# Pair chunks of a GLU kernel: seven products with the left-over rows stacked in, weight sums in another order, a PSUM bank seeded by a copy

## The chip, the cores and the metric

The kernel runs on one core of one Trainium2 chip. The metric is the time of one execution in microseconds (us); it is given as the median of several runs, and smaller is better. PE is the matrix engine (PEld its weight loads), DVE the vector engine, ACT the scalar engine, POOL the GpSimd engine (it issues the DMAs that add into DRAM), SP the sync engine (it issues most loads). Each engine works through its own queue in the order in which the program was laid out.

## The reference

```python
h  = x + A_ref(layernorm(x), wqkv, wo)          # attention over 8 dilated keys, 32 heads
def B_ref(x, w_gate, w_up, w_down):
    h = sigmoid(x @ w_gate) * (x @ w_up)        # x: 2048 x 576, F = 4608
    return h @ w_down
h2 = h + B_ref(layernorm(h), w_gate, w_up, w_down)
```

All is float32. The second half, the GLU, takes most of the time and is all that the change touches.

## The kernel before

**Precision.** A float32 operand is split into a high part (rounded to fp32r) and a low part (what is left), and a product of two operands is three matmuls: high times high, low times high, high times low. `split` (L103) is one ACT copy for the high part and one DVE subtraction for the low part.

**Tiling.** The 2048 tokens are four blocks of 512. F is cut into 36 pieces of 128. The contraction of 576 is 512 (four slabs of 128, two *halves* of two slabs) and a *rest* of 64. The rest's high and low parts are stacked on 128 partitions, so that a rest costs two matmuls (`rest`, L751) and not three.

**Chunks.** The list `items` has 84 chunks, numbered c: 12 single chunks of block 0, 24 *pair chunks* of blocks 0 and 1 (c = 12 to 35), 12 single chunks of block 2 (c = 36 to 47), and 36 pair chunks of blocks 2 and 3 (c = 48 to 83, "the last pair"). A pair chunk (`pair`, from L818 on) computes gate and up of both blocks with seven block products in place of eight: the blocks' halves are a00, a01 (first block), a10, a11 (second), and with sums s1 to s4 of them and sums t1 to t4 of the weights the products are b00, b10, t2, t3, t1, t4 and b11, each of six matmuls (`prod`, L742), accumulated in three PSUM banks b1, b2, b3. Four rests of two matmuls go with b10, t1, t4 and b11. That makes 50 matmuls of 512 columns a chunk. Between products, partial results are copied (ACT) or added (DVE), with a high priority; the gate of the first block is copied out of b1 (L824), the product b10 is added by DVE (L829), and ACT takes the sigmoid (L830).

**Work between the products.** `between(i)` puts other work after each product: down projections of earlier chunks, and one step of a background generator. In the last pair the down projection also has seven products (`down_seven`, L919): 42 matmuls of 288 columns a chunk, PSUM tile `dp`, evicted by ACT into `ev` (L936), and added to DRAM by a POOL DMA (L939). In single chunks `dp` is added to `stage` by DVE (L878).

**Weights.** `weights` (L712) makes the operands of chunk c+1 while chunk c runs: DVE sums (L727 to L730) into a tile `tw`, then splits into w1 (two buffers), w2, w3, w4 (one each). `load_gu` (L700) loads the raw weights of chunk c+2 into `wg` (two buffers, SP); it can start when the last reader of the buffer is done. `down_side` (L1153) loads the raw down weights `wd` of two chunks, splits them, and sums them.

**Operands of the last pair.** During the single chunks c = 36 to 47 the background generator makes blocks 2 and 3 of the GLU's input (`proj_scr`, tiles `ar` and `ar3`), and `operands` (L1014) then makes the sums (`sums`, L279) and their splits (`x_half`, L300) in a pool `pp2`, c = 45 to 46. At c = 48 the last two operands, s1 and a11, are split, `pp2` is closed, and `wd` takes its place in SBUF.

**Order.** No order is written out by hand: a scheduler places the instructions of all engines by its own estimates, with priorities (`tc.high_priority`) and pins (`tc.issue_after`). So an edit in one place can move instructions elsewhere.

## Time and profile before

| | |
|---|---|
| median of 3 runs | 1569.44 us (1567.49 to 1575.35) |
| profiled execution: span from first to last instruction | 1566.1 us (no other time is given for it) |
| single chunks of block 2 | about 746 to 938 us |
| last pair, c = 48 to 83 | about 938 to 1536 us, then the last down products |
| weights in wg of the last pair | 36 loads of 640 KB |

A row of a timeline reads: start in us, duration in us, engine, line, operation, out<-in, shape, count of merged instructions, and in brackets the idle time before it with what ended it. PE's ends are modelled (matmuls are pipelined), so PE is read by the distance from start to start. The same goes for DVE and ACT, where one instruction's end overlaps the next one's start by some 0.1 us.

### The profile page before, as it was taken

The numbers are of one execution on the slowest core, as the hardware profiler recorded it, in microseconds if no ns is written. First come the engines' busy times: TensorE is split into PE (matmuls) and PEld (weight loads), VectorE is DVE, ScalarE is ACT, GpSimd is POOL, SyncE is SP. The second block draws the span as 40 slices with busy tenths as digits, with TensorE's granted clock in tenths as the row PEclk, the third lists the DMA queues.
The fourth block names the chain that finished last, engine by engine and source line by source line (L and its number), as shares of the span: only waits on it lengthen the run. The fifth ranks groups of instructions, "written<-read, shape, count | busy, mean of one in ns | idle before, by whom it ended". The sixth has DMA issues, their size and how long they took to land.

```text
span 1566.1 us, 22356 instructions
## 1 busy us (share of the span) xinstructions
PE 1545.8 (99%) x8520; PEld 1374.2 (88%) x8520; DVE 1254.3 (80%) x1880; ACT 882.6 (56%) x1584; POOL 207.4 (13%) x252
## 2 busy tenths in 40 slices
PE   8999999999999999999999999999999999999998
PEld 7999988887888888888888988888888888888888
DVE  7998999979999999999536688866777776677754
ACT  6632344435566555665542355766777666677761
POOL 3300000011000010000101000121112112112212
PEclk9999999999999999999999999999999999999999
DMA  8646555366565775665683424998899989989983
GB/s 281 219 166 222 190 200 183 107 225 199 145 174 150 200 183 150 162 159 125 180 243 113 179 85 119 205 180 176 170 181 186 172 172 183 175 170 181 185 166 137
DMA packets 77148, 273.96 MB, mean 175 GB/s; under 512 B 8336, under 2 KB 14224, under 8 KB 76144
## 3 DMA queue, kind: packets, MB, share of 16 engines
q0 software_dynamic: 28192, 107.29, 37.4%
q1 hardware_dynamic: 41216, 145.11, 27.8%
q10 hardware_dynamic: 7632, 20.12, 3.3%
q8 instruction: 66, 1.08, 0.3%
q14 instruction: 42, 0.34, 0.1%
HBM read 143.98 MB, written 130.87 MB: 176 GB/s over the span
## 4 chain that ended last, share of the span: by engine, by line
PE 82%; DVE 10%; DMA 5%; ACT 2%; issue 1%; POOL 0%; SPq 0%; ACTq 0%; POOLq 0%; DVEq 0%
PE b L747 40%; PE dp L868 14%; PE dp L930 11%; PE b L754 8%; PE acc L157 4%; DMA wg<-in_wmlp_dram 2%; DVE pr L189 2%; DVE lg L193 1%; DVE pr L215 1%; PE b L157 1%; PE bgp L157 1%; DMA x<-tok 1%; DVE w L105 1%; DMA kw<-k 1%; DVE pr L221 1%
## 5 line engine op out<-in xcount | busy, mean ns | idle before, releaser
L747 PE MATMUL b<-tl,w 128*128 128x512 f32 x1692 | 429.6, 393 | 1.2 <-ACT s L824 0.6
L747 PEld LDWEIGHTS b<-tl,w 128*128 128x128 f32 x1692 | 305.8, 188 | 57.9 <-ACT tl L104 1.2
L747 PE MATMUL b<-th,w 128*128 128x512 f32 x1332 | 343.0, 392 | 0.5 <-DVE s L843 0.5
L747 PEld LDWEIGHTS b<-th,w 128*128 128x128 f32 x1332 | 242.7, 188 | 45.3 <-DVE s L843 0.9
L936 ACT ACTIVATE ev<-dp 128x576 f32<-128x576 f32 x224 | 145.0, 647 | 62.9 <-PE dp L930 58.6
L754 PE MATMUL b<-th,w 128*128 128x512 f32 x564 | 174.9, 391 | 0.0
L939 POOL DMA_DIRECT2D h<-ev x128 | 109.2, 853 | 459.4 <-ACT ev L936 445.6
L104 ACT ACTIVATE w<-wg 128x384 fp32r<-128x384 f32 (+1 forms) x186 | 111.0, 600 | 98.5 <-PE b L754 54.4
L157 PE MATMUL acc<-qw,th 128*128 128x432 f32 x512 | 154.5, 363 | 2.4 <-DVE th L109 2.3
L105 DVE TENSOR_TENSOR w<-wg,w 128x384 fp32r<-128x384 f32 (+1 forms) x186 | 121.0, 656 | 36.7 <-ACT w L104 36.5
L105 DVE TENSOR_TENSOR w<-tw,w 128x512 fp32r<-128x512 f32 x120 | 82.6, 688 | 81.6 <-ACT w L104 80.7
L754 PEld LDWEIGHTS b<-th,w 128*128 128x128 f32 x564 | 106.0, 188 | 23.0
L868 PE MATMUL dp<-d,h1h 128*128 128x288 f32 x640 | 118.8, 295 | 0.0
L868 PE MATMUL dp<-d,h0h 128*128 128x288 f32 x608 | 112.2, 295 | 0.0
L876 ACT ACTIVATE stage<-dp 128x576 f32<-128x576 f32 x104 | 66.9, 646 | 68.1 <-PE dp L868 67.8
L157 PEld LDWEIGHTS acc<-qw,th 128*128 128x128 f32 x512 | 96.9, 189 | 7.7 <-DVE th L109 3.1
L868 PEld LDWEIGHTS dp<-d,h1h 128*128 128x128 f32 x640 | 98.7, 189 | 3.0
L868 PEld LDWEIGHTS dp<-d,h0h 128*128 128x128 f32 x608 | 94.0, 189 | 3.5 <-DVE stage L878 0.3
L104 ACT ACTIVATE w<-tw 128x512 fp32r<-128x512 f32 x120 | 75.3, 628 | 35.7 <-PE b L747 34.6
L157 PE MATMUL acc<-qw,tl 128*128 128x432 f32 x256 | 92.8, 363 | 0.1
L189 DVE TENSOR_TENSOR pr<-kw,q 128x2304 f32<-128x2304 f32 x32 | 81.8, 2555 | 8.3 <-DMA kw<-k 8.1
L884 POOL DMA_DIRECT2D h<-stage x26 | 31.1, 1197 | 416.2 <-ACT stage L876 337.2
(323 smaller groups left out, 2969.6 us busy)
## 6 DMA issues: line engine op xcount, KB each, us to landing
h<-ev POOLq DMA_DIRECT2D x96, 576.0 KB, 7.3
wg<-in_wmlp_dram SPq DMA_DIRECT2D x47, 928.0 KB, 5.2
h<-stage POOLq DMA_DIRECT2D x26, 1152.0 KB, 11.6
wg<-in_wmlp_dram SPq DMA_DIRECT2D x36, 640.0 KB, 4.2
kw<-k SPq DMA_DIRECT2D x16, 792.0 KB, 4.6
vw<-v SPq DMA_DIRECT2D x16, 792.0 KB, 4.9
wd<-in_wmlp_dram SPq DMA_DIRECT2D x18, 576.0 KB, 7.2
h<-ev POOLq DMA_DIRECT2D x32, 288.0 KB, 6.8
```

What stands on the lines that cost most here:

```text
L104: act.activation(hi, src, AF.Copy)
L105: splits.append(dve.tensor_tensor(lo, src, f32(hi), ALU.subtract))
L157: pe.matmul(ps[:, :n], a[:, c, js], m[:, c], start=k == 0, stop=False)
L189: dve.tensor_tensor(pr, both(kw, u), q[:, us].unsqueeze(2).broadcast_to([P, 2, W, CG]), ALU.mult)
L747: pe.matmul(ps, wt[:, a, k0 + c], xx[:, m + c], start=first and k == 0, stop=k == 5, skip_group_check=True)
L754: pe.matmul(ps, wt[:, a, k0], xx[:, 4], start=False, stop=a == 1, skip_group_check=True)
L868: pe.matmul(ps[:, i, :DH2], a[:, js], d[:, m, i * DH2:(i + 1) * DH2], start=k == 0, stop=k == n)
L876: act.activation(hv, ps, AF.Copy)
L884: pool.dma_start(hacc[b], hs, accum_op=ALU.add, max_dma_last_dim=8 * D)
L930: pe.matmul(ps[:, i, :DH2], a[x][:, js], m[y], start=k in (0, 1, 3) and q == 0, stop=q == 2, skip_group_check=True)
L936: act.activation(hs[:, k % 2], ps[:, :, :DH2], AF.Copy)
L939: pool.dma_start(hsev[:, u, k0:k + 1], hs[:, :k + 1 - k0], accum_op=ALU.add, max_dma_last_dim=8 * D)
```

## The change

1. **49 matmuls.** In the last pair, the rest takes part in the seven products: each half of the contraction is now 256 + 32, the 32 rows stand four times on the 128 partitions (x: high, low, high, low; weights: high, high, low, low), so that one matmul gives all of it. Seven products of six, and seven rests of one: 49 matmuls. The weights come from a second array `wfull`, 1536 columns a chunk in place of 1280 (768 KB in place of 640 KB).
2. **Weight sums and splits of the last pair** (`full_weights`) are made in place in `wg`, in another order, over 384 columns each; the rests of t1 to t4 lie in one tile `tr`. Its first split (w1) is pinned on ACT behind the sigmoid of the chunk before.
3. **Operands of the last pair.** The rests of blocks 2 and 3 go through DRAM (`rscr`) and come back fourfold in sixteen POOL DMAs (`rr`), their sums are made separately (`sums_rest`, five DVE additions), and `x_full` splits all seven operands with their rests (`split_quads`: one ACT copy, two DVE subtractions on 32 partitions each). Before, three operands had a rest, with one subtraction each.
4. **Order of products and PSUM seeding, all pair chunks.** b00, t3, t2, b10, t1, t4, b11. Except in the first chunk of each pair (c = 12 and 48), ACT copies b00 into the bank of b10 (`b2`), b10 is accumulated on it, and ACT takes the sigmoid from there: the DVE addition of L829 is gone. The bank of b00 is the one that held b10 in the chunk before.
5. **The second block's gating** is placed ahead of b11 (`last(1, ...)`), the first one's behind it.
6. Buffers: `s` 3 (4), `ev` 3 (4), `d3` 1 (2).

```diff
+    def split_quads(t, src):
+        act.activation(t, src, AF.Copy)
+        for q in (32, 96):
+            dve.tensor_tensor(t[q:q + 32], src[q:q + 32], f32(t[q:q + 32]), ALU.subtract)
...
+    def sums_rest(q0, q1, s1):
+        (a00, a01), (a10, a11) = q0, q1
+        dve.tensor_tensor(s1, a10, a11, ALU.add)
+        yield
+        dve.tensor_tensor(a10, a00, a10, ALU.subtract)
+        yield
+        dve.tensor_tensor(a00, s1, a00, ALU.subtract)
+        yield
+        dve.tensor_tensor(a01, a01, a00, ALU.subtract)
+        yield
+        return dict(s1=s1, s2=a00, s3=a10, s4=a01, a11=a11)
...
+    def full_weights(ws):
...
+            w1 = gw.tile([P, 2, 5, P], F32R, bufs=2, name="w1")
+            with ExitStack() as way:
+                if c >= NF + NSTD:
+                    way.enter_context(tc.issue_after(added[1]))
+                act.activation(w1[:, :, 0:3], r[:, 2:4], AF.Copy)
...
+            dve.tensor_tensor(r[:, 1], r[:, 0], r[:, 1], ALU.subtract)
+            dve.tensor_tensor(r[:, 2], r[:, 1], r[:, 2], ALU.add)
+            dve.tensor_tensor(r[:, 3], r[:, 3], r[:, 2], ALU.subtract)
+            tr = gw.tile([P, 8, P], F32R, tag="tw", name="tr")
+            w2 = sum_pair("w2", 0, slice(1, 3))
...
+            act.activation(w4[:, 0:3], r[:, 0], AF.Copy)
...
+            dve.tensor_tensor(r[:, 0], r[:, 0], r[:, 2], ALU.subtract)
+            w3 = sum_pair("w3", 2, slice(0, 4, 3))
...
-        prod(b2, X["a01"], w, "b10", True)
-        rest(b2, X["a01"], w, "g4")
...
-            added[0] = dve.tensor_tensor(s1, s1, b2, ALU.add)
-            act.activation(s1, s1, AF.Sigmoid)
+        product(b1, "b00", "a00", w, True, ())
...
+            act.activation(b2 if clean else s1, b1, AF.Copy)
...
+        product(b3, "t3", "s3", w, True, ())
...
+        product(b1, "t2", "s2", w, False, ())
...
+        product(b2, "b10", "a01", w, not clean, (("a01", "g4"),))
...
+            if clean:
+                act.activation(s1, b2, AF.Sigmoid)
...
+            for i in range(2):
+                for h in range(2):
+                    a = rscr[i][32 * h:32 * h + 32, :]
+                    for q in range(4):
+                        pool.dma_start(rr[i][h][32 * q:32 * q + 32], a)
```

How the scheduler's order changes is shown at three places. The first is PE in the first chunk of the last pair (c = 48) and the start of the next. Before, from the product t1 of chunk 48 on (tl_9019 is s1, th_9022 is a11, th_8904 is s4, tl_8832 is a00):

```order
L747 MATMUL b1_9049<-tl_9019,w3_8941 128x512 x6
L754 MATMUL b1_9049<-th_9022,w4_8939 128x512 x2
L747 MATMUL b3_9051<-th_9022,w3_8941 128x512 x6
L754 MATMUL b3_9051<-th_9022,w1_8936 128x512 x2
L747 MATMUL b1_9049<-th_8904,w4_8939 128x512 x6
L754 MATMUL b1_9049<-th_8904,w4_8939 128x512 x2
L747 MATMUL b2_9212<-tl_8832,w1_9031 128x512 x6
```

After, from the product b00 of chunk 49 (bank b1_9258) on; xs3, xs2 and xs1 are the rests of s3, s2 and s1, tl_9047 is s1, th_9054 a11, th_8994 s4, tl_8970 s3:

```order
L822 MATMUL b1_9258<-tl_8859,w1_9064 128x512 x6
L832 MATMUL b1_9258<-xa00_8860,w1_9064 128x512
L832 MATMUL b3_9090<-xs3_8971,tr_8944 128x512
L822 MATMUL b3_9090<-th_9054,w3_8955 128x512 x2
L832 MATMUL b2_9089<-xs2_8988,tr_8944 128x512
L822 MATMUL b3_9090<-th_9054,w3_8955 128x512 x4
L822 MATMUL b2_9089<-tl_9047,w3_8955 128x512 x6
L832 MATMUL b2_9089<-xs1_9048,tr_8944 128x512
L832 MATMUL b3_9090<-th_9054,tr_8944 128x512
L822 MATMUL b2_9089<-th_8994,w4_8950 128x512 x6
L832 MATMUL b2_9089<-th_8994,w4_8950 128x512
L822 MATMUL b3_9259<-tl_8970,w2_9072 128x512 x6
```

Ahead of these rows PE has, from the start of chunk 48, b00 with its rest (7), the six of t3, the six of t2, and b10 with its rest (7), with 46 matmuls of `dp` between them. The rest matmuls of t3 and t2 have moved behind all of that and behind b00 of the next chunk.

The second place is DVE in chunk 48. Before, from the gating of the last single chunk (L767) to the rest of a11 (L109):

```order
L767 TENSOR_TENSOR s_8970<-s_8970,b2_8955 128x512
L878 TENSOR_TENSOR stage_7678<-stage_7678,dp_9005 128x576
L105 TENSOR_TENSOR h1l_9002<-s_8970,h1h_9001 128x512
L105 TENSOR_TENSOR w4_8939<-wg_8855,w4_8939 128x384
L105 TENSOR_TENSOR th_9022<-ar3_8328,th_9022 128x1024
L878 TENSOR_TENSOR stage_7678<-stage_7678,dp_9062 128x576
L105 TENSOR_TENSOR w1_9031<-wg_8952,w1_9031 128x640
L727 TENSOR_TENSOR tw_9037<-wg_8952 128x512
L829 TENSOR_TENSOR s_9052<-s_9052,b2_9050 128x512
L109 TENSOR_TENSOR th_9022<-ar3_8328,th_9022 64x512
```

After, the same gating (L850) is followed by nineteen rows (four of `stage`, two of 1024 columns, the weights of chunks 48 and 49 and the rest of a11 among them) and then by these; s_9092 is the gate of chunk 48, whose addition needs b10:

```order
L924 TENSOR_TENSOR s_9092<-s_9092,b1_9091 128x512
L107 TENSOR_TENSOR w2_9072<-wg_8960,w2_9072 128x2x256
L965 TENSOR_TENSOR stage_7657<-stage_7657,dp_9172 128x576
L770 TENSOR_TENSOR wg_9087<-wg_9087 128x384
L304 TENSOR_TENSOR rd_8815<-rr10_8818,rr11_8819 128x512
L306 TENSOR_TENSOR rr10_8818<-rr00_8816,rr10_8818 128x512
L116 TENSOR_TENSOR xs1_9048<-rd_8815,xs1_9048 32x512 x2
L116 TENSOR_TENSOR xs3_8971<-rr10_8818,xs3_8971 32x512 x2
L308 TENSOR_TENSOR rr00_8816<-rd_8815,rr00_8816 128x512
L310 TENSOR_TENSOR rr01_8817<-rr01_8817,rr00_8816 128x512
L116 TENSOR_TENSOR xs2_8988<-rr00_8816,xs2_8988 32x512 x2
L116 TENSOR_TENSOR th_8994<-rr01_8817,th_8994 32x512 x2
```

The sums and splits of the rests stand behind the addition that waits for b10. On ACT, in chunk 49, the split of the first down weights (d3<-wd) stands ahead of the first gating's copy (h0h) and of the seeding copy (L909).

The third place is DVE in every second chunk further on. Before, between the last read of a raw weight buffer (w4<-wg_12213) and the first read of the weights loaded into it (w1<-wg_12556) stood these rows:

```order
L105 TENSOR_TENSOR w4_12393<-wg_12213,w4_12393 128x384
L728 TENSOR_TENSOR tw_12546<-wg_12406,tw_12546 128x256
L105 TENSOR_TENSOR h0l_12526<-r00_12523,h0h_12525 128x512
L730 TENSOR_TENSOR tw_12546<-wg_12406,tw_12546 128x256
L829 TENSOR_TENSOR s_12561<-s_12561,b2_12559 128x512
L105 TENSOR_TENSOR w2_12544<-tw_12546,w2_12544 128x512
L843 TENSOR_TENSOR s_12563<-s_12563,b1_12558 128x512
L105 TENSOR_TENSOR d_12659<-wd_12236,d_12659 128x576
L848 TENSOR_TENSOR s_12562<-s_12562,b3_12560 128x512
L105 TENSOR_TENSOR w3_12545<-tw_12546,w3_12545 128x512
L105 TENSOR_TENSOR w1_12733<-wg_12556,w1_12733 128x640
```

After, the last read is tr<-wg_10231, and the first read of what is loaded into its place is the sum on wg_10584 (L770); s_10591 and s_10590 are the additions that wait for the products t1 and t4:

```order
L107 TENSOR_TENSOR w3_10424<-wg_10231,w3_10424 128x2x256
L753 TENSOR_TENSOR tr_10413<-wg_10231,tr_10413 64x256
L772 TENSOR_TENSOR wg_10429<-wg_10429 128x384
L107 TENSOR_TENSOR w2_10569<-wg_10429,w2_10569 128x2x256
L770 TENSOR_TENSOR wg_10584<-wg_10584 128x384
L929 TENSOR_TENSOR s_10591<-s_10591,b1_10586 128x512
L933 TENSOR_TENSOR s_10590<-s_10590,b3_10587 128x512
```

Only two rows are now left between the end of the buffer's use and the first read of its next load, and the additions stand behind that read.

More of the change, by code (lines that the diff above doesn't have):

```diff
@@ L45 @@
 GU = 10 * P
+GF = 12 * P
 WC = GU + D
@@ L60, with kernel @@
 @with_exitstack
-def kernel(ctx, tc, x, wqkv, wo, wmlp, out):
+def kernel(ctx, tc, x, wqkv, wo, wmlp, wfull, out):
     nc = tc.nc
@@ L298, in tl_tile, with x_full @@
         return xt.tile([P, 4, TB], F32R, tag="tl", bufs=4, name="tl")
+    def x_full(n, raw, rest):
+        if n in ("a01", "a11", "s4"):
+            t = th_tile()
+            r = t[:, 4]
+        else:
+            t = tl_tile()
+            r = xr.tile([P, TB], F32R, name="x" + n)
+        split(t[:, 0:2], t[:, 2:4], raw)
+        split_quads(r, rest)
+        XR[n] = r
+        return t
+    XR = {}
+    xr = None
     def x_half(raw, rest):
@@ L746, in prod, with product @@
             for a, m in ((0, 0), (0, 2), (1, 0)):
-                pe.matmul(ps, wt[:, a, k0 + c], xx[:, m + c], start=first and k == 0,
+                lhs = wt[:, a, k0 + c] if isinstance(k0, int) else wt[:, 2 * a + c]
+                pe.matmul(ps, lhs, xx[:, m + c], start=first and k == 0,
                           stop=k == 5, skip_group_check=True)
                 k += 1
+    def product(ps, n, xn, w, first, rests):
+        prod(ps, X[xn], w, n, first)
+        if isinstance(w[n][1], int):
+            for m, wn in rests:
+                rest(ps, X[m], w, wn)
+        else:
+            pe.matmul(ps, w[n][1], XR[xn], start=False, stop=True, skip_group_check=True)
     def rest(ps, xx, w, n):
@@ L849, in pair @@
             gated[0] = act.activation(s2, s2, AF.Sigmoid)
+            added[1] = getattr(gated[0], "ins", gated[0])
         between(5)
-        prod(b1, X["s4"], w, "b11", False)
-        rest(b1, X["s4"], w, "u4")
         with tc.high_priority(HC):
-            last((s1, b1), (s2, s3))
+            last(1, s2, s3)
+        product(b1, "b11", "s4", w, False, (("s4", "u4"),))
+        with tc.high_priority(HC):
+            last(0, s1, b1)
         between(6)
@@ L1292, in between @@
                 side(i)
-            pair(X, w, between, last)
+            pair(w, between, last)
         else:
@@ L1309, in between @@
                 down_side(f, i)
-            pair(X, w, between, last if f >= NF - NPL else last_sums(f))
+            pair(w, between, last if f >= NF - NPL else last_sums(f))
             if f < NF - NPL:
```

133 lines of the change are left out of this document (88 added, 45 removed).

## The prediction

> **What bounds the kernel now.** I read the page's busy line first, then PE's waits, then the windows by stage.
>
> ```profile
> PE 1545.8 (99%) x8520; PEld 1374.2 (88%) x8520; DVE 1254.3 (80%) x1880; ACT 882.6 (56%) x1584; POOL 207.4 (13%) x252
> ```
>
> A busy PE need not be a PE at its limit, so what it waits for is asked next. In the pair chunks it waited three times, 1.6 us in all:
>
> ```profile
> PE b L747 <- ACT s L824: 0.6, 1, 0.6
> ```
>
> ```profile
> PE b L747 <- DVE s L843: 0.5, 1, 0.5
> PE b L747 <- ACT tl L104: 0.5, 1, 0.5
> ```
>
> The windows of the last pair, its start and its long part. The columns are the length, then the busy time of PE, PEld, DVE, ACT and POOL with their instructions, the granted clock, the DMA share and GB/s:
>
> ```profile
> 938.00:985.00 47.00, 47.00 (x243) 40.63 (x241) 41.74 (x73) 26.15 (x48) 2.99 (x3) 1.00 0.53 134
> 985.00:1510.00 525.00, 525.00 (x2823) 458.72 (x2822) 376.90 (x651) 374.05 (x658) 104.88 (x123) 1.00 0.91 179
> ```
>
> The last pair is bound by PE from end to end, at the full clock. In its long part DVE has 28% to spare (377 of 525 us) and ACT 29%; in its first 47 us DVE has 11%. So a matmul less is time gained, and DVE work costs nothing in the long part but may cost at the start.
>
> **The change, part by part.** The sums below are made on the profiled execution (span 1566.1 us) and then taken off or put on the median of 1569.44, which lies 3.3 us above it.
>
> *49 matmuls.* The price of one is read from start to start, at the rests and in the product ahead of them:
>
> ```profile
> 1109.29 1.55 PE L747 MATMUL b<-tl,w 128*128 128x512 f32 x6
> 1110.67 0.62 PE L754 MATMUL b<-th,w 128*128 128x512 f32 x2
> 1111.14 0.29 PE L930 MATMUL dp<-d,h0h 128*128 128x288 f32 x1
> ```
>
> Six take 1.38 us, the two rests 0.47: 0.23 each. 36 chunks lose one each: 36 x 0.23 = **8.3 us less**. The rows of "128*128" do not say how many rows hold data, and the stacked rest is the same 128x512 as the old one, so it is priced alike. [...]
>
> *DVE addition gone, seeding.* Some 58 additions of 512 columns go. PE did not wait for them (rows above), so they are worth nothing by themselves; what covers them is PE's own work between b10 and the second gating. The seeding copy is as long as the copy that it replaces. It now waits for the gating of the chunk before, which reads its bank; between that chunk's b11 and the product t2, which needs the copy done, PE has b00, t3 and at least one `dp` group, over 3 us.
>
> *The start of the last pair.* Here the order was moved most. The rows around 938 us in the trace of before give the spacing of DVE's operations by size, where DVE ran without a gap:
>
> ```profile
> 934.87 0.69 DVE L105 TENSOR_TENSOR w<-tw,w 128x512 fp32r<-128x512 f32 x1
> 935.47 1.22 DVE L105 TENSOR_TENSOR tl<-rs,tl 128x1024 fp32r<-128x1024 f32 x1
> 936.61 0.68 DVE L767 TENSOR_TENSOR s<-s,b 128x512 f32<-128x512 f32 x1
> ...
> 938.66 0.55 DVE L105 TENSOR_TENSOR w<-wg,w 128x384 fp32r<-128x384 f32 x1
> 939.13 1.22 DVE L105 TENSOR_TENSOR th<-ar,th 128x1024 fp32r<-128x1024 f32 x1
> 940.27 0.75 DVE L878 TENSOR_TENSOR stage<-stage,dp 128x576 f32<-128x576 f32 x1
> 940.93 0.82 DVE L105 TENSOR_TENSOR w<-wg,w 128x640 fp32r<-128x640 f32 x1
> ...
> 958.58 0.43 DVE L728 TENSOR_TENSOR tw<-wg,tw 128x256 f32<-128x256 f32 x1
> 958.92 0.76 DVE L105 TENSOR_TENSOR d<-wd,d 128x576 fp32r<-128x576 f32 x1
> ```
>
> From start to start: 0.60 for 512 columns, 1.14 for 1024, 0.47 for 384, 0.66 for 576, 0.34 for 256. Half the partitions do not make it shorter:
>
> ```profile
> 942.98 0.69 DVE L109 TENSOR_TENSOR th<-ar,th 64x512 fp32r<-64x512 f32 x1
> ```
>
> so I price the new ones on 32 partitions at 0.60 too. Up to the last single chunk's gating (L767 at 936.61) both orders hold nearly the same DVE work, because the new operations ahead of it replace ones that have moved behind; I let it start at 936.7. From it to the split of the rest of s3 (xs3) the new order has 14 operations of 512 columns, 5 of 576, 2 of 1024, 5 of 384, 3 of 256 and one smaller: 8.4 + 3.3 + 2.3 + 2.4 + 1.0 + 0.2 = 17.6 us. So the rest of s3 is there at **954.3**.
>
> PE's work up to there is counted from the start of chunk 48:
>
> ```profile
> 936.64 1.54 PE L747 MATMUL b<-tl,w 128*128 128x512 f32 x6
> 938.02 0.42 PE L868 MATMUL dp<-d,h1h 128*128 128x288 f32 x2
> ...
> 939.61 1.54 PE L747 MATMUL b<-th,w 128*128 128x512 f32 x6
> ```
>
> Twelve `dp` matmuls take 939.61 - 938.02 = 1.59 us, 0.13 each. The new order gives PE 7 + 6 + 6 + 7 matmuls of chunk 48, b00 of chunk 49 (7) and 46 of `dp`: 33 x 0.23 + 46 x 0.1325 = 13.7 us, that is until **950.3**. Then it meets the rest of t3 and waits 4.0 us. Behind that it has three matmuls (0.7 us) until the rest of t2, for which DVE needs two sums and two splits, 2.4 us: 1.7 us more, until 956.7.
>
> A third wait follows in chunk 49. The first load of down weights (`wd`) began in the run of before as soon as the last split that read `pp2`'s space had ended (935.47 + 1.22):
>
> ```profile
> 936.76 0.90 SPq L1145 DMA_DIRECT2D wd<-in_wmlp_dram x2
> ```
>
> From the issue of these two to landing:
>
> ```profile
> DMA to landing us min/median/max: 3.9/4.4/4.9
> ```
>
> Now that space holds the fourfold rests, and the reader that ends last is the split of xs2, at 956.7. With 3.9 to 4.9 us to land (the answer just quoted, for these two transfers) the weights are there at 961. ACT's rows of 512 columns give its spacing:
>
> ```profile
> 956.04 0.60 ACT L824 ACTIVATE s<-b 128x512 f32<-128x512 f32 x1 [0.22 <-PE b L747]
> 956.53 0.62 ACT L104 ACTIVATE h0h<-r 128x512 fp32r<-128x512 f32 x1
> ```
>
> ACT wants the down weights at about 962.6: t4 ends at 959.7 (956.7 and 13 matmuls), then come two additions (1.2), the sigmoid and two weight copies at 0.55 each, an estimate from these two rows (0.49 from start to start, 0.60 alone). Behind the down weights stand the gating's copy and the seeding copy, done at 964.2. PE has finished b11 and t3 by 962.9 and wants to write t2 over the seeded bank: 1.3 us of waiting. Together 4.0 + 1.7 + 1.3 = **7.0 us more**.
>
> The bounds take the times from issue to landing by kind of transfer (median us, last column):
>
> ```profile
> h<-ev POOLq DMA_DIRECT2D x96, 576.0 KB, 7.3
> ...
> wg<-in_wmlp_dram SPq DMA_DIRECT2D x36, 640.0 KB, 4.2
> ...
> wd<-in_wmlp_dram SPq DMA_DIRECT2D x18, 576.0 KB, 7.2
> ...
> h<-hj POOLq DMA_DIRECT2D x12, 288.0 KB, 2.6
> ```
>
> At least: the rest of s3 cannot come before b10's end (947.1) and the eight rows from the addition to xs3 (ten operations, 5.9 us), 953.0, so 2.7 + 1.7 = 4.4 us. At most: the down weights land in the 7.2 us that all loads of `wd` take in the median and not in 3.9 (+1.3), and DVE comes 3 us later than I let it, since every one of its microseconds counts there: 11.5 us.
>
> ```profile
> 903.82 0.74 POOL L976 DMA_DIRECT2D h<-hj  x1 [2.04 <-DVE hj L262]
> ```
>
> ```profile
> 916.18 0.26 ACT L978 ACTIVATE ar<-bgp 128x128 f32<-128x128 f32 x1
> ```
>
> The sixteen POOL transfers are covered. The last column of `ar` is written at 916.44, a POOL issue takes 0.74, so the write and eleven loads behind it are out by 926; the nearest POOL transfers land 2.6 (h<-hj) to 7.3 us (h<-ev) later, over 12 us ahead of their first use on DVE (946).
>
> *The long part.* A chunk gets some 1.6 us more of DVE work on weights and loses 0.6; it has 4.8 us of DVE to spare (28% of a chunk's 17.1 us, which are 50 x 0.23 + 42 x 0.1325). The new rest tile and the in-place sums put the first read of a load two rows behind the end of the buffer's last use. 768 KB at the pace of 640 in 4.2 us take 5.0, so DVE stands for some 4 us at that sum. In the order shown third, the buffer's last use comes some 7.5 us after t4 of the chunk before: b11 ends 2.4 us after it (a `dp` group of 0.8, seven matmuls of 1.6), and eleven DVE rows follow (5 us). The addition behind the waiting sum needs t1, which ends 14.4 us after that t4 (six products of 1.6, six groups of 0.8): the load is hidden up to 6.9 us, and with the 2 us until b11 needs the addition, up to 9. I price it at nothing.
>
> ```profile
> 1101.91 0.85 POOL L939 DMA_DIRECT2D h<-ev  x1 [5.10 <-ACT ev L936]
> ```
>
> ```profile
> 1109.71 0.64 ACT L936 ACTIVATE ev<-dp 128x576 f32<-128x576 f32 x1
> ```
>
> With three `ev` buffers, a buffer is written 7.8 us after the issue of its last transfer (1109.71 - 1101.91), against 7.3 to land; ACT may stand for a moment, and `dp`'s second bank covers some 4 us.
>
> *Blocks 0 and 1.* The start of their pair (350 to 390 us) has the 1.6 us of waits quoted first; with s3 wanted ahead of s2 they may vanish or double: 0, from -1.6 to +1.6.
>
> Sum: -8.3 + 7.0 = -1.3, **1568 us**.
>
> **The rivals.** (1) *The gain stays whole.* The rests are ready by 950, PE never waits: 1569.4 - 8.3 = 1561. Against it stands the order: the splits of xs3 are behind an addition that needs b10. (2) *The start costs more* than the gain: `wd` or DVE late as in the upper bound and beyond, each microsecond passing straight to PE: -8.3 + 11.5 or more, 1573 and up. For it speaks that DVE is at 89% there already. (3) *Slower: a load of weights holds up DVE in every second chunk.* If 768 KB take longer than 9 us from the last use of the buffer, the additions behind the waiting sum come late, b11 waits, and so does the rest of t3. Each microsecond beyond 9 costs 18: at 10 us 1568 + 18 = 1586. Against it: the 640 KB loads take 4.2; for it: a DMA share of 0.91 and `wd` at 7.2. (4) *PE is not the bound*, something paces it: then the removal gives nothing and the start costs 7, 1576. The even 0.23 from start to start speaks against. [...]
>
> **How the numbers follow.** My forecast has 0.62 (1564 to 1572), the whole gain 0.13, a dearer start 0.13 (a third of it above 1577), the held load 0.09, PE not the bound 0.03. 0.5% is 7.8 us, about what a measurement of this kernel tells from no change: faster means below 1561.6, slower above 1577.3. That gives 0.13 faster, 0.13 slower (0.04 + 0.09), 0.74 same. The range of 1560.5 to 1576 holds the forecast, with its bounds (1563.9 at -8.3 + 4.4 - 1.6 and 1574.2 at -8.3 + 11.5 + 1.6), the whole gain, two thirds of the dearer start and the fourth rival: 0.87; without the whole gain it would be 0.74, too little.
>
> **What would show it.** Right: 36 matmuls fewer; PE with two gaps in chunk 48 whose releaser is L116, and one in chunk 49 on ACT's seeding copy; `wd`'s first issue 20 us later than before; chunk pairs of the long part shorter by 0.46 us. Wrong: no gap near 950; PE waits that recur after 985; a rest matmul that takes more than 0.23.

## The result, and the profile after

| | before | after |
|---|---|---|
| median of 5 runs each | 1569.55 us (1567.49 to 1575.35) | 1580.27 us (1577.52 to 1583.76) |
| ratio of the runs, 95% interval | | 1.0062 (1.0046 to 1.0078) |
| profiled execution, span | 1566.1 us | 1577.0 us |

The change made the kernel slower by 0.6%, where no difference was forecast. The busy line of the page after:

```profile
PE 1543.8 (98%) x8484; PEld 1368.7 (87%) x8484; DVE 1300.6 (82%) x2016; ACT 907.4 (58%) x1660; POOL 216.7 (14%) x270
```

There are 36 matmuls fewer, as intended, and PE is still busy 98% of the span. That share hides what happened. The windows of the last pair (length, busy time of PE, PEld, DVE, ACT and POOL, granted clock, DMA share, GB/s) show it:

```profile
938.00:985.00 47.00, 38.97 (x181) 31.00 (x180) 43.03 (x75) 22.11 (x40) 1.27 (x1) 0.93 0.33 84
985.00:1510.00 525.00, 523.12 (x2817) 456.67 (x2816) 431.27 (x800) 397.57 (x732) 104.92 (x122) 1.00 0.93 187
```

Before, PE was busy for all of both stretches. Now 8 of the first 47 us are empty, the clock in them is 0.93 on average, and 1.9 us are empty in the long part. PE's waits after, in the blocks and the last pair:

```profile
PE b L832 <- DVE xs L116: 4.1, 1, 4.1
PE b L822 <- DVE s L929: 2.8, 4, 1.5
PE b L153 <- DVE tl L107: 2.1, 1, 2.1
PE b L822 <- DVE s L850: 1.4, 1, 1.4
...
PE bgp L157 <- DVE th L111: 1.2, 1, 1.2
PE b L822 <- ACT s L913: 1.0, 1, 1.0
```

For the ledger, the same points of the work are compared in both profiles: the first product b00 of chunks 48, 51 and 82, PE's last gate or up matmul, and its last matmul of all. Of these, the starts of chunks 51 and 82 on PE after:

```profile
995.43 0.62 PE L822 MATMUL b<-tl,w 128*128 128x512 f32 x2
...
1521.31 0.62 PE L822 MATMUL b<-tl,w 128*128 128x512 f32 x2
```

And before:

```profile
980.32 0.62 PE L747 MATMUL b<-tl,w 128*128 128x512 f32 x2
...
1510.82 0.39 PE L747 MATMUL b<-tl,w 128*128 128x512 f32 x1
```

| stretch | before | after | difference |
|---|---|---|---|
| up to chunk 48 | 936.6 | 942.2 | +5.5 |
| chunks 48 to 50 | 43.7 | 53.3 | +9.6 |
| chunks 51 to 81 | 530.5 | 525.9 | -4.6 |
| the last two chunks | 25.0 | 24.6 | -0.3 |
| the last down products | 25.7 | 26.5 | +0.9 |

The rows add up to 11 us. An undisturbed chunk takes 16.89 us and took 17.11, so the 31 chunks alone should have gained 7.0; 2.4 of that was lost again in two of them.

The head of the last pair, on PE after. In brackets stands the idle time and what ended it:

```profile
942.16 1.65 PE L822 MATMUL b<-tl,w 128*128 128x512 f32 x6 [1.39 <-DVE s L850]
...
955.06 1.65 PE L822 MATMUL b<-tl,w 128*128 128x512 f32 x6 [0.56 <-DVE s L924]
956.55 0.40 PE L832 MATMUL b<-xa,w 128*128 128x512 f32 x1
961.03 0.77 PE L832 MATMUL b<-xs,tr 128*128 128x512 f32 x1 [4.08 <-DVE xs L116]
962.81 1.22 PE L822 MATMUL b<-th,w 128*128 128x512 f32 x2 [1.01 <-ACT s L913]
963.83 0.77 PE L832 MATMUL b<-xs,tr 128*128 128x512 f32 x1
964.39 1.87 PE L822 MATMUL b<-th,w 128*128 128x512 f32 x4
966.10 1.55 PE L822 MATMUL b<-tl,w 128*128 128x512 f32 x6
```

The forecast wait for the rest of s3 (xs) is there, 4.1 us. DVE's rows say where the operand was:

```profile
941.42 0.68 DVE L850 TENSOR_TENSOR s<-s,b 128x512 f32<-128x512 f32 x1
...
954.32 0.69 DVE L924 TENSOR_TENSOR s<-s,b 128x512 f32<-128x512 f32 x1
...
959.50 1.38 DVE L116 TENSOR_TENSOR xs<-rr,xs 32x512 fp32r<-32x512 f32 x2
```

DVE had no gap between these rows; the rest of s3 stood behind the addition that needs b10 (L924), as in the order. Behind PE's wait the four matmuls at 964.39 are 0.43 apart, not 0.23. The window gives the reason; the number before the DMA share is the granted clock:

```profile
961.00:966.00 5.00, 3.96 (x8) 2.60 (x9) 4.03 (x6) 2.23 (x4) 0.00 (x0) 0.50 0.95 187
```

After the 4 us pause PE ran at half its clock until 966: eight matmuls at 0.20 us extra, 1.6 us. The same happened at 826 to 829.5, in the background work for block 3, behind a wait of 2.13 us that had been 1.88 before; with the wait itself that stretch became 1.8 us longer. By the trace's granted clock the half clock lasted here from 959.27 to 966.10, 6.83 us, and there from 826.15 to 829.56, 3.41 us. The first began 2.3 us into the pause of 4.1 us, the second 0.4 us behind the end of the pause of 2.13 us (825.77). The last section sets the pause at 823 us in fourteen profiles beside the clock that followed it.

### The profile page after: what moved, and what is told of

Its sections match the earlier page's. It is cut to its first block, busy times and chain, and to the rows that moved or that the text cites. A ratio compares the mean times of both kernels' runs of the same rounds, so it can differ in the third digit from the quotient of the medians.

```text
span 1577.0 us, 22464 instructions
## 1 busy us (share of the span) xinstructions
PE 1543.8 (98%) x8484; PEld 1368.7 (87%) x8484; DVE 1300.6 (82%) x2016; ACT 907.4 (58%) x1660; POOL 216.7 (14%) x270
## 4 chain that ended last, share of the span: by engine, by line
PE 72%; DVE 16%; DMA 5%; issue 3%; ACT 2%; POOL 1%; ACTq 0%; POOLq 0%; DVEq 0%; SPq 0%
PE b L822 35%; PE dp L955 13%; PE dp L1017 9%; PE acc L164 4%; PE b L837 3%; PE b L832 3%; DVE pr L196 2%; DMA wg<-in_wmlp_dram 2%; DVE lg L200 1%; DVE pr L222 1%; PE b L164 1%; DVE w L107 1%; PE bgp L164 1%; DVE stage L965 1%; DMA kw<-k 1%
## 5 line engine op out<-in xcount | busy, mean ns | idle before, releaser
L822 PE MATMUL b<-th,w 128*128 128x512 f32 x1332 | 345.3, 394 | 3.8 <-DVE s L929 2.8
L822 PEld LDWEIGHTS b<-th,w 128*128 128x128 f32 x1332 | 243.2, 188 | 50.5 <-DVE s L929 3.6
L106 ACT ACTIVATE w<-wg 128x384 fp32r<-128x384 f32 (+2 forms) x186 | 111.5, 602 | 106.3 <-PE b L837 34.1
L107 DVE TENSOR_TENSOR w<-wg,w 128x384 fp32r<-128x384 f32 (+2 forms) x186 | 121.3, 656 | 42.3 <-ACT w L106 41.8
L837 PE MATMUL b<-th,w 128*128 128x512 f32 x276 | 85.6, 390 | 0.0
L222 DVE TENSOR_TENSOR pr<-vw,lg 128x2304 f32<-128x2304 f32 x32 | 81.8, 2556 | 0.8
L200 DVE TENSOR_REDUCE lg<-pr 128x128 f32<-128x2304 f32 x32 | 81.6, 2550 | 0.3
L770 DVE TENSOR_TENSOR wg<-wg 128x384 f32<-128x384 f32 x36 | 20.0, 556 | 69.9 <-DMA wg<-in_wfull_dram 69.9
## 6 DMA issues: line engine op xcount, KB each, us to landing
h<-stage POOLq DMA_DIRECT2D x26, 1152.0 KB, 11.5
```

The source lines that it names most:

```text
L106: act.activation(hi, src, AF.Copy)
L107: splits.append(dve.tensor_tensor(lo, src, f32(hi), ALU.subtract))
L200: dve.tensor_reduce(lg[:, us].rearrange("p j w h -> p (j w h)"), pr.rearrange("p j w (h d) -> p (j w h) d", d=DH), AX.X, ALU.add)
L222: dve.tensor_tensor(pr.rearrange("p j w (h d) -> p j w h d", d=DH), both(vw, u).rearrange("p j w (h d) -> p j w h d", d=DH), lg[:, us].uns ...
L822: pe.matmul(ps, lhs, xx[:, m + c], start=first and k == 0, stop=k == 5, skip_group_check=True)
L837: pe.matmul(ps, wt[:, a, k0], xx[:, 4], start=False, stop=a == 1, skip_group_check=True)
```

## The experiments

Theory A was that the loss sits at the head of the last pair, because DVE has more work there than it had: A1 that the place of the rests in its queue is what counts, A2 that its total is. The rivals were that order and seeding cost by themselves (D), that other things would be as late without the rests (B, E), and later a reuse of SBUF space (F). The runs were measured in three groups, e1 to e4, e5 to e8 and e9 to e12, each beside the kernel before; its medians there were 1570.73, 1570.97 and 1570.31 us.

| run | median, us | ratio to before, 95% interval |
|---|---|---|
| e1_pool | 1587.02 | 1.0105 (1.0085 to 1.0125) |
| e2_prio | 1580.81 | 1.0062 (1.0044 to 1.0080) |
| e3_onesub | 1575.35 | 1.0029 (1.0017 to 1.0042) |
| e4_ordseed | 1572.65 | 1.0011 (0.9999 to 1.0022) |
| e5_norest | 1573.48 | 1.0014 (0.9998 to 1.0030) |
| e6_firstone | 1576.19 | 1.0033 (1.0017 to 1.0048) |
| e7_noseed | 1584.76 | 1.0086 (1.0071 to 1.0102) |
| e8_before | 1570.81 (one run) | |
| e9_dk | 1571.18 | 0.9994 (0.9980 to 1.0008) |
| e10_dkpin | 1570.30 | 0.9990 (0.9974 to 1.0006) |
| e11_dkhalf | 1594.97 | 1.0127 (1.0094 to 1.0161) |
| e12_onedk | 1575.18 | 1.0036 (1.0019 to 1.0054) |

**Order and seeding alone (e4_ordseed).** The kernel after, with `weights`, `x_half` and `operands` of before for the last pair:

```diff
-            wc = (full_weights(wg) if c + 1 >= NF + NSTD else
-                  weights(items[c + 1][0], wg))
+            wc = weights(items[c + 1][0], wg, c + 1 < NF + NSTD)
...
-                    Xn[n] = x_full(n, *raw[n])
+                    Xn[n] = x_half(*raw[n])
```

> The new order of products, the seeding, the second gating ahead of b11 and the smaller buffers, but the last pair with its old operands, old weights and 50 matmuls. Theory A (the loss is in the operands and weights of the 49 matmuls): the time of the kernel before, 1567 to 1572, and PE's waits at the start of the last pair under 2 us. Theory D (order and seeding cost by themselves, in all 60 pair chunks or ahead of the last pair, where the changed kernel had lost 3.7 us by 938): 1573 or more, with the 3.7 us there again.

Measured 1572.65, 1.9 us above before and short of a clear difference; it lies between the bounds of the two theories (1572 and 1573). In its profile, of one of its faster executions (1568.82), chunk 48 starts at 936.96, so the 3.7 us are not there, the three chunks take 45.1 us, and no chunk from 51 to 81 is disturbed. Order and seeding alone thus cost some 2 us (none to 3.5 by the interval); most of the loss comes with the 49 matmuls' operands and weights. A chunk with 50 matmuls takes 17.08 us in this run, 0.03 less than before.

**The rests on POOL (e1_pool).**

```diff
-        dve.tensor_tensor(s1, a10, a11, ALU.add)
+        pool.tensor_tensor(s1, a10, a11, ALU.add)
...
-            dve.tensor_tensor(t[q:q + 32], src[q:q + 32], f32(t[q:q + 32]), ALU.subtract)
+            pool.tensor_tensor(t[q:q + 32], src[q:q + 32], f32(t[q:q + 32]), ALU.subtract)
```

> The changed kernel with the four sums of the rests and the fourteen subtractions of their splits on POOL instead of DVE; nothing else. It takes 18 operations of 0.60 us, 10.8 us, out of DVE's queue between 925 and 966 us, and PE's order has the rest of t3 and of t2 again right behind their products. Theory A (the loss sits at the head of the last pair, because DVE's queue there is too long and the rests stand late in it): the waits of PE at 940 (1.4 us), 956 (4.1) and 961 (1.0) and the half clock behind them (1.6) go, 8 us in all, so about 1572. Theory B (the rests are not what is late; the weights and the gating would be as late without them): under 3 us gained, 1577 or more. Theory C (POOL is too slow for it: its sum of 128x1152 took 2.81 us, so about 1.25 us each of these): the rest of t3 still late, a wait of several us on POOL.

Measured 1587.02: worse than the change by 6.8 us, which none of the theories expected. DVE in that run, and then POOL beside it:

```profile
935.19 0.55 DVE L772 TENSOR_TENSOR wg<-wg 128x384 f32<-128x384 f32 x1
...
942.16 1.61 DVE L770 TENSOR_TENSOR wg<-wg 128x384 f32<-128x384 f32 x1
943.70 2.28 DVE L107 TENSOR_TENSOR tl<-rs,tl 128x1024 fp32r<-128x1024 f32 x1
945.90 0.68 DVE L850 TENSOR_TENSOR s<-s,b 128x512 f32<-128x512 f32 x1
```

```profile
941.76 1.59 POOL L310 TENSOR_TENSOR rr<-rr,rr 128x512 f32<-128x512 f32 x1
943.43 6.97 POOL L116 TENSOR_TENSOR xs<-rr,xs 32x512 fp32r<-32x512 f32 x4
```

The 384-column sums took 0.55 us with POOL idle and 1.61 beside a POOL operation; 1024 columns took 2.28 in place of the 1.22 quoted in the prediction. L850, which reads one operand from PSUM, kept its 0.68. The 18 operations (four sums, for `sums_rest` holds four additions and not five, and fourteen subtractions) left DVE's queue, but sixteen others that ran beside POOL took 0.4 to 1.1 us more each, 15 us in all against the 10.8 saved, and the gating of the last single chunk came at 945.9, so PE waited 7.7 us for it. So the two operations shown with both inputs in SBUF took 1.06 us more each beside POOL, and L850, with an operand in PSUM, no more than elsewhere. Why is not shown.

**The rests' sums with priority (e2_prio).**

```diff
-            rq = yield from sums_rest(*rr, rd)
+            with tc.high_priority(HI):
+                gen = list(sums_rest_now(*rr, rd))
+            rq = gen[0]
```

(`sums_rest_now` lays down the four sums in one step.)

> The changed kernel with the four sums of the rests at the priority of the splits, so that they and the splits of the rests of s3 and s2 stand on DVE ahead of the addition that waits for b10 (27 rows earlier). The same work for DVE. Theory A1 (the place in the queue is what costs): the 4.1 us wait goes, and most of the half clock with it: 5 to 6 us gained, about 1575. Theory A2 (DVE's total work between 905 and 966 us is the bound, whatever comes first): the wait moves to the splits of the halves or to the gatings of the last single chunks, and less than 2 us are gained, 1578 or more.

Measured 1580.81, against 1580.27: nothing gained. PE in that run:

```profile
962.81 0.50 PE L840 MATMUL b<-th,tr 128*128 128x512 f32 x1 [0.57 <-DVE th L116]
964.22 1.63 PE L830 MATMUL b<-tl,w 128*128 128x512 f32 x6 [0.91 <-DVE s L941]
969.03 0.80 PE L840 MATMUL b<-xs,tr 128*128 128x512 f32 x1 [3.18 <-DVE tr L761]
```

PE no longer waits for the rests of s3 and s2. It waits for what they were moved ahead of: the rest of a11, the addition of t4, and 3.2 us for the rests of the weights of chunk 49 (tr), with twelve matmuls at half clock behind that. The last wait was not made by DVE's work: on DVE tr stands right behind the first tile r of the hidden activations, and that stood 3.8 us for a DMA:

```profile
967.83 0.69 DVE L1303 TENSOR_TENSOR r<-s,b 128x512 f32<-128x512 f32 x1 [3.76 <-DMA h<-stage]
968.55 0.42 DVE L761 TENSOR_TENSOR tr<-wg,tr 64x256 fp32r<-64x256 f32 x1
```

So the time is what A2 expected, but this run does not decide between A1 and A2. The wait of r, theory F, is taken up at e5.

**One subtraction per split (e3_onesub).**

```diff
-        for q in (32, 96):
+        for q in (32,):
...
+                    pool.memset(rr[i][h][96:128], 0.0)
-                    for q in range(4):
+                    for q in range(3):
```

> The changed kernel with the rests stacked high, low, high, zero: one subtraction per split instead of two (the product of low with low part of the rest is left out), and twelve loads instead of sixteen. Seven operations of 0.60 us leave DVE, five of them ahead of the end of the split of s2's rest: a00, a01, a11, s3 and s2. The order is else as in the changed kernel. Theory A2 (DVE's total work is the bound) expects the rest of s3 2.4 us earlier and that of s2 3.0 us earlier: about 1577, and below if the wait falls under the 2 us at which PE's clock stayed whole. Theory A1 (place in the queue): the rests still stand behind the addition that needs b10, whose end PE's own work sets, and only the subtractions behind it count: 1 to 1.5 us, 1579.

Measured 1575.35: 4.9 us less than the change for 4.2 us less work on DVE, with the order as it was. A2 had said 3 and had left room for the clock (its 2 us are the pause of 1.88 us in the profile of before, behind which the clock was 1.00; behind e11's of 1.86 it was 0.50, as the last section has it); in the profile PE no longer waits for the rest of s3, but 0.2 to 1.8 us in six other places.

**No work on the rests (e5_norest).**

```diff
-        for q in (32, 96):
-            dve.tensor_tensor(t[q:q + 32], src[q:q + 32], f32(t[q:q + 32]), ALU.subtract)
...
-        dve.tensor_tensor(s1, a10, a11, ALU.add)
+        return dict(s1=a10, s2=a00, s3=a10, s4=a01, a11=a11)
```

> The changed kernel with all of DVE's work on the rests left out: no sums of the rests, and splits of rests that are the copy alone (so their low parts and sums are not computed). The 49 matmuls, loads, copies and all else stay. Eighteen operations of 0.60 us, 10.8 us, leave DVE between 925 and 966 us, as in the run with POOL, but with nothing on POOL beside them. Theory A2 (DVE's total work at the head of the last pair is the bound) expects PE's waits from 940 to 975 and the half clock to go but for about 2 us, and the single wait at 1009 with them: 1580.3 less 10 to 13, 1567 to 1570. Theory E (not DVE but the loads of 768 KB, the weights' splits or the down weights are late as well) expects 1573 or more, with waits on tr, w or h0h in their place.

Measured 1573.48, 3.5 to 6.5 us more than A2 expected, so part of theory E holds. PE in this run, at the head and in the long part:

```profile
963.53 0.61 PE L1008 MATMUL dp<-d,h0h 128*128 128x288 f32 x1 [3.97 <-ACT h0h L106]
...
1347.60 2.54 PE L813 MATMUL b<-th,w 128*128 128x512 f32 x6 [3.87 <-DVE s L920]
```

And DVE ahead of each:

```profile
961.52 0.69 DVE L1284 TENSOR_TENSOR r<-s 128x512 f32<-128x512 f32 x1 [3.19 <-DMA h<-stage]
...
1346.38 0.56 DVE L761 TENSOR_TENSOR wg<-wg 128x384 f32<-128x384 f32 x1 [9.53 <-DMA wg<-in_wfull_dram]
```

The first is a wait that the rests had hidden: the tile `r` of the hidden activations lies in the space of the last `stage` tile, whose POOL DMA landed 8.8 us after its issue in the change's profile. The second is the forecast's third rival, in single chunks: a load of weights that landed so late that the addition behind the waiting sum, and PE, stood still. PE waited so in three chunks of this profile, 0.6, 1.4 and 3.9 us. In the profile of the change the same thing cost 1.5 us at 1011 and 0.4 at 1079.

**Rests first, one subtraction (e6_firstone).** Both edits of e2 and e3, and `sums_rest` ahead of `sums`.

> One subtraction per split (as in the run with twelve loads; the product of low with low parts of the rests is left out) and the sums of the rests with the priority of the splits, ahead of the sums of the halves. Theory A2: with the same total work for DVE as with one subtraction alone, the place in the queue is worth less than 2 us: 1574 to 1577. Theory A1 (place in the queue decides once the total is lower): 1571 or less.

Measured 1576.19, the time that A2 expected. Again the wait of r on the stage tile was the next one, on DVE:

```profile
969.45 0.69 DVE L1305 TENSOR_TENSOR r<-s 128x512 f32<-128x512 f32 x1 [4.72 <-DMA h<-stage]
```

PE stood 5.9 us behind it, and ten matmuls ran at half clock.

**The tiles moved (e9_dk),** on top of e6:

```diff
-                    for n in ("s4h", "s4l", "s1h"):
+                    for n in ("s4h", "s4l", "s1h", "s1l", "s2h", "s2l", "s3h", "s3l"):
```

> The kernel with one subtraction per split and the rests first (the product of low with low parts of the rests is left out), and eight instead of three tiles of the pool for the hidden activations laid down ahead of r, so that r no longer lies where the last stage tile lay. In the run without this edit DVE's first r<-s waited 4.7 us for the DMA that reads that tile, PE 5.9 us behind it, and ten matmuls at half clock followed (2.0). Theory F (this reuse of space is the wait that is next once the rests are early): PE's wait at 965 goes with the half clock, 6 to 8 us: 1568 to 1570. Theory A2 alone (DVE's total work is the only bound): under 2 us, 1574 or more.

Measured 1571.18, 5.0 us less than e6. DVE and the windows of the last pair in this run:

```profile
966.21 0.69 DVE L1305 TENSOR_TENSOR r<-s 128x512 f32<-128x512 f32 x1
```

```profile
938.00:985.00 47.00, 45.13 (x223) 37.15 (x222) 46.12 (x83) 28.96 (x53) 1.27 (x1) 1.00 0.38 104
```

The wait is gone and the clock whole; DVE is now busy 46.1 of 47 us. Chunks 48 to 50 take 46.6 us, 6.7 less than in the change and 3.6 more than before less three matmuls. Theory F holds where the rests come first.

**The same without rests first (e12_onedk):** e3 with the moved tiles.

> One subtraction per split, the sums of the rests in the place that the change gave them, and the tiles of the hidden activations moved. Theory A2 and F together expect the wait for the DMA of the last stage tile (2.0 us on DVE, 1.8 on PE, nine matmuls at half clock) to go: 1575.4 less 2 to 4, 1571 to 1573, and above the run with the rests first and the same tiles by up to 3 us, because waits on the rests remain.

Measured 1575.18, as e3: nothing gained. ACT in this run:

```profile
965.37 1.01 ACT L106 ACTIVATE d<-wd 128x288 fp32r<-128x288 f32 x2 [3.94 <-DMA wd<-in_wmlp_dram]
```

Here the down weights are late, as in the upper bound of the prediction's third wait: their space comes free only behind the splits of the rests, they took 7.5 us to land, and what stands behind them on ACT waits too. So F's wait is the next one only where the rests, and with them the down weights, are early. Read the other way, e9 and e12 differ in the place of the rests alone, and e9 is 4.0 us faster, with intervals that do not meet. The place in the queue (A1) does count, once the wait of r behind it is gone; in e2 and e6 that wait had hidden it.

**The first sum pinned (e10_dkpin),** on top of e9:

```diff
-            dve.tensor_tensor(r[:, 1], r[:, 0], r[:, 1], ALU.subtract)
+            with ExitStack() as way:
+                if c >= NF + NSTD:
+                    way.enter_context(tc.issue_after(getattr(added[0], "ins", added[0])))
+                dve.tensor_tensor(r[:, 1], r[:, 0], r[:, 1], ALU.subtract)
```

> The run before this one, and the first in-place sum on a newly loaded weight buffer pinned on DVE behind the addition that waits for t4, so that a late load no longer holds up the additions of t1 and t4. The third rival of the prediction, in single chunks instead of in every second one: such loads cost 1 to 8 us an execution (in the run without rest work 1.6, 4.0 and 0.7 us of PE's waits ahead of t4, all of PE on the addition of t1); with the pin they go: 2 to 4 us less than that run, and a smaller spread. If the sums come too late for w2 instead, chunk periods rise above 16.89.

Measured 1570.30, 0.9 less than e9, which their intervals do not tell apart; the runs spread from 1564.5 to 1574.2, and from 1568.2 to 1577.4 without the pin. In its profile no wait of PE in the long part is on the additions, but five chunks are 0.2 to 1.2 us longer, three of them with a wait on ACT's seeding copy. The cost of the late loads has moved and is not gone.

**Two transfers a load (e11_dkhalf),** on top of e9:

```diff
-        behind[0] = sp.dma_start(ws[:, :n], src[f][:, :n])
+            sp.dma_start(d4[:, 1:3], s4[:, 1:3])
+            behind[0] = sp.dma_start(d4[:, 0:4:3], s4[:, 0:4:3])
```

> The run with the moved tiles, and each load of weights of the last pair in two transfers, the two middle quarters and then the two outer ones, so that the first can start when the splits of w2 are done and only 384 KB are left for the end. If the late loads are late because they start late (behind the last read of the buffer), DVE's idle time ahead of the first sum falls from 1.9 us a chunk to under 1 us and the waits of PE at the additions go: 2 to 4 us less than the run with the moved tiles. If they are late because the DMA engines are busy (share 0.95), nothing changes.

Measured 1594.97, 23.8 us more than e9, where a gain or no change was expected. SP's waits in the long part say why the first transfer did not help:

```profile
SPq L748 <- DVE tr L766: 387.7, 31, 19.4
```

It still waits for the last reader of the whole buffer (tr), so both start together. DVE's waits for the loads grew from 69.9 to 82.8 us, and PE's on the additions behind them from 0.6 to 10.7, with half clock behind four of these. Of the 31 pairs 6 landed more than 7.3 us after their first issue, of e9's 31 loads only 1. Why is not shown, and whether an earlier start would help was not tried.

**Without the seeding (e7_noseed).**

```diff
-        order[:] = [n2, n1, n3, True]
+        order[:] = [n2, n1, n3]
```

> The changed kernel without the seeding: b10 starts its bank anew in every pair chunk, and DVE adds b00's copy to it, 0.60 us more on DVE in 58 chunks, among them two more ahead of 980 us. The prediction's step (the addition is covered by PE's own work in the long part): 1579 to 1582, chunk periods of 16.89 us as before the edit. Against it (the seeding is what DVE's lower load or PE's waits hang on): 1584 or more, with periods above 16.9.

Measured 1584.76, 4.5 us more than the change, where 0 to 2 were expected; measured against the kernel before of each group it is 3.8 us, and the two intervals still overlap a little (1.0046 to 1.0078 and 1.0071 to 1.0102). The chunk's median is 16.91 in place of 16.89, six chunks are disturbed (5.9 us together), the last two with the down products behind them take 2.9 us more, and the head 2.5. The runs do not say which of these belongs to the addition and which to the order that the scheduler then chose.

**Before, again (e8_before).**

> The kernel before, once more, for a second profile: the first product of the single chunks of block 0 started at 218.96 us in the first profile of it and at 219.7 to 220.9 in the five of changed kernels, whose order up to there is the same on every engine. If that is scatter between executions, this profile lies between 219 and 221; if it belongs to the changed program, it lies at 219.0 again.

Its first single chunk starts at 221.32 us, in place of 218.96, and all up to chunk 48 lies 2.4 to 2.7 us later. So the 1.2 us that the change had lost by its own start of that chunk are within the scatter between executions.

## Why the prediction was wrong, point by point

- **A matmul less: right.** 17.11 - 16.89 = 0.22 to 0.23 a chunk, 8.1 us for 36, against 8.3. The stacked rest takes no longer than another matmul (0.22 to 0.24 us from its start to the next, in the change). The seven rows of a product are evenly 0.23 apart as before. By e4, 0.03 of it belongs to the new order and the seeding, which no term of the sum held.
- **The start: the mechanism right, its size too small.** 7.0 us were forecast. Chunks 48 to 50 lost 9.6 and should have won 0.7, and chunk 48 began 1.8 us late: 12.1. So the second rival came true, the start that costs more than the gain. (Its bound adds up to 7.0 + 1.3 + 3 = 11.3 us and not 11.5; 12.1 lies beyond both.) Three steps failed:
  - The first is "I let it start at 936.7": the new work ahead of the gating does not just replace what moved behind it. L850 came at 941.4, 4.8 us later than before; 3.7 us of that is what all the rest had lost by then, and the remaining 1.1 with the order of PE's work gave the wait of 1.4 us.
  - The second is the chain to the rest of s3, 17.6 us forecast, 19.5 measured (941.4 to 960.9). Its operations were counted rightly, but eleven of the fourteen of 512 columns came 0.70 to 0.73 us apart and not 0.60. The row of 64 partitions that the forecast quotes (942.98) already had its successor 0.72 behind it.
  - The third is missing from the sum altogether: half a clock behind a long wait, 1.6 us.

  The wait for xs3 itself, 4.1 us against 4.0, agreed only by luck, because PE too was late, by 6.5 us. The second wait, 1.7 us for the rest of s2, did not come; in its place PE stood 1.0 us for ACT's copy of t3 (L913), whose bank t4 needs. PE's waits in chunks 48 to 50 add up to 6.6 us and the half clock to 1.6; some 2 us of the loss there are in neither and stay open.
- **The third wait** was forecast as 1.3 us on ACT's own rows, with the down weights in time, and PE stood 0.4 in the change (L909). Late down weights, its upper bound, show in e12, 3.9 us on ACT. What I had not seen is the tile r in the space of the stage tile, which came out as soon as the rests were early or gone from DVE (e1, e2, e5, e6).
- **The long part, "I price it at nothing": wrong by 2.4 us in the profile.** DVE stands for the load in every second chunk, as forecast (69.9 us in 16 waits, 4.4 each, against "some 4 us"). But I had taken the median of the landing times, and the usual place of the issue, where the longest and the latest decide. From issue to landing in the long part, after, and then in e5:

```profile
DMA to landing us min/median/max: 4.2/5.1/7.1
```

```profile
DMA to landing us min/median/max: 4.1/5.2/11.2
```

  A load is usually issued 6.0 us after the start of its chunk. In nine profiles (the change, e1, e2, e3, e5, e6, e7, e9, e12) no load that DVE stood for and that landed up to 13.2 us after that start made PE wait, and each that landed at 13.5 us or later did. So some 7.3 us from issue to landing are hidden: the forecast's 6.9 was near, its outer bound of 9 too wide. In e5 loads of 8.7 and 11.2 us went beyond. In the change none did from the usual place, and its longest, 7.1 us, was hidden. The two that PE waited on took 6.6 us, but were issued 8.3 and 7.1 us after the start of their chunks. The first of them on DVE and PE, and then the one of 7.1 us:

```profile
1010.37 0.56 DVE L770 TENSOR_TENSOR wg<-wg 128x384 f32<-128x384 f32 x1 [4.23 <-DMA wg<-in_wfull_dram]
...
1011.58 0.73 PE L822 MATMUL b<-th,w 128*128 128x512 f32 x2 [1.52 <-DVE s L929]
```

```profile
1382.45 0.56 DVE L770 TENSOR_TENSOR wg<-wg 128x384 f32<-128x384 f32 x1 [5.36 <-DMA wg<-in_wfull_dram]
```

  From 970 to 1006 us DVE had no gap of more than 0.15 us: it was still behind from the head, and freed the buffer late. Issued at the usual place, loads of 6.6 us would have been hidden. So in this profile the loss in the long part is an after-effect of the start, and rival 3 happened in two chunks in place of every second.
- **The seeding "worth nothing by itself": not confirmed.** Taking it out cost some 4 us (e7), of which the addition and the changed order can't be told apart.
- **Up to chunk 48:** 0 with 1.6 either way was forecast, for the start of blocks 0 and 1, which held. The 5.5 us lie elsewhere: 1.1 ahead of 820 (scatter, by e8), 1.8 at 823 to 832 (mostly half clock, which followed that pause in five of fourteen profiles), 0.8 near 880 (a wait on DVE L111, 1.2 us), 1.8 at chunk 48.
- **The last down products:** 0.9 us, not in the sum. DVE's last product of two SBUF tiles (L850) ran beside POOL's addition of the tails:

```profile
1546.23 1.76 DVE L850 TENSOR_TENSOR s<-s 128x512 f32<-128x512 f32 x1 [0.70 <-ACT s L934]
```

  Before, it took 0.71, and POOL's addition began 1.1 us behind it; after, POOL began 1.5 us ahead of it (1544.77). Why POOL came earlier is not shown.

```profile
1535.78 0.71 DVE L767 TENSOR_TENSOR s<-s 128x512 f32<-128x512 f32 x1 [0.70 <-ACT s L849]
```

Together: -8.1 + 12.1 + 2.4 + 0.9 + 3.7 = 11.0. The forecast had found the chain of waits at the start, priced its links too low, and summed the first ones alone.

No version beat the kernel before clearly: e9 and e10 lie at 0.999 of it with intervals that hold 1. Of what keeps them from the 8 us, e9's profile shows 3.6 us at the head; the late loads take a part that differs by execution, and how much the rest is scatter stays open.

## What to carry to other kernels

Where an engine that is not the bound has no room for a while (DVE at 89% of 47 us here), price every operation added there at its full length, and then ask what is late next: here rests, weights, down weights and a reused tile stood in a row, and mending one showed the next. A load that must come in time is judged by its longest landing and by its latest issue, and not by the median of either. And an engine that looks idle is no free place: POOL took 10.8 us of work from DVE and slowed DVE's other work by 15.

## What the runs showed of the hardware

- **PE's clock fell to half behind some short pauses and not behind others of the same length.** The wait at 823 us is in all fourteen profiles, 1.72 to 2.13 us long. The 3.00 us from 0.6 us behind its end on are compared. In five profiles they had a granted clock of 0.50 (0.57 in e10) and 14 to 16 matmuls: behind the pauses of 1.86 (e11), 1.88 (e9), 2.08 (e10), 2.09 (e3) and 2.13 us (the change). In nine they had 1.00 and 25 matmuls: behind 1.72 (e1), 1.76 (e7), 1.80 (e2), 1.82 (e5), 1.85 (e6), 1.88 (before), 1.89 (e8), 1.93 (e4) and 2.03 us (e12). So the length of the pause alone did not decide, for 1.88 us stands on both sides; what did is not shown. In the change's profile the half clock lasted 3.41 us at 826.15 and 6.83 us at 959.27. The stretch that holds most of the pause and the one behind it, in the change and then in e12; the granted clock is the number before the DMA share:

```profile
822.74:826.15 3.41, 1.28 (x9) 0.90 (x9) 2.99 (x5) 3.04 (x6) 0.00 (x0) 1.00 0.31 70
826.15:829.56 3.41, 3.41 (x17) 3.41 (x16) 1.12 (x3) 1.33 (x2) 0.00 (x0) 0.50 0.98 392
```

```profile
821.70:825.12 3.42, 1.70 (x10) 1.20 (x8) 2.81 (x5) 3.42 (x7) 0.00 (x0) 1.00 0.34 95
825.12:828.53 3.41, 3.10 (x24) 3.10 (x25) 2.39 (x4) 1.11 (x3) 0.00 (x0) 1.00 0.89 346
```

- **DVE took longer beside POOL** where both worked on tiles of SBUF: 0.4 to 1.1 us more for each of sixteen DVE operations (e1), and 1.05 for one of 512 columns (1.76 against 0.71, the tail). L850 with an operand in PSUM took 0.68 us beside POOL (e1), as in the change.
- **Loads of 768 KB** on a DMA share of 0.93 landed in 4.1 to 11.2 us with a median of 5.1 to 5.2 (the change and e5); 640 KB before, on a share of 0.91, in 3.8 to 6.0, median 4.4.
